# Where two batches of attention pairs are finished: moving pairs 12 and 13 of a fused retention and SwiGLU kernel behind the second tile's first quad

## The chip, the cores and the metric

The kernel runs on one core of one Trainium2 chip. Its engines are TensorE (PE in the profile, its weight loads PEld), VectorE (DVE), ScalarE (ACT), GpSimd (POOL) and SyncE (SP), which issues DMAs. Each engine works off its own instructions in order; an instruction waits for semaphores of the others. ScalarE and SyncE also issue DMAs, each in its own queue, marked ACTq and SPq. The metric is the time of one execution in microseconds (us), as a median over runs.

## The reference

Two blocks follow one another. First retention (attention without softmax) over 8 batches, 8 heads, 576 positions and head size 64:

```python
scores = (1 / sqrt(64)) * (q @ k.T)
gamma = 1 - 2.0 ** (-5 - head)
ret = scores * where(i >= j, gamma ** (i - j), 0)
attn = ret @ v
```

Its output becomes x, 4608 tokens of 512 features (heads side by side). Then a SwiGLU feed-forward block with 1536 hidden features:

```python
g = x @ w_gate
out = ((g * sigmoid(g)) * (x @ w_val)) @ w_out
```

q, k and v come as 32-bit floats, the three weights as 64-bit floats, which the kernel rounds to 32 bits itself.

## The kernel before, in words

**Pairs and ticks.** Retention is done for two heads at a time: 8 batches of 4 such pairs, 32 in all. A pair goes through three stages, and `tick(t)` (L482) does one stage for each of three pairs: for pair t-2 the values (`own_values`, `earlier_values`, `to_x`), for pair t-1 the states and scores (`new_states`, `scores`, `masked`), for pair t the transposes of q and k by VectorE and the scaling of kn by ScalarE (`transposes`, L402 and L404). Inside a tick TensorE does new_states, own_values, earlier_values and scores, and VectorE follows with to_x, masked and the two transposes. new_states writes the PSUM tile that masked of the tick before reads. A tick takes only pairs in the bounds that it is given (`lo`, `hi`).

**Loads.** `load(i)` (L248) fetches pair i: 14 DMAs by SyncE, eight for q and k, two for kn, four for v. `next_load(t)` asks for pair t+2.

**Tiles.** The feed-forward block takes the tokens in tiles: tile 0 has 512 tokens, tiles 1 to 4 have 1024. A tile needs the pairs of all batches that it touches: `needed(1)` is 14, so tile 1 needs pairs 0 to 11, whose last stage is in tick 13. Ticks for later pairs are spread among a tile's steps.

**Tile 0** is plain matmul: `up0(f, ...)` (L496) makes hidden block f of 12 in two PSUM banks (A and B, or C and E, in turn), `down0(f)` (L511) adds block f's part of the output in all four banks, and `out0` (L516) copies the banks out, three by VectorE and bankE by ScalarE (L522). Between the up0 calls VectorE rounds the weights (L372 to L375). The ticks 4 to 9 stand there at places written out in a table (`tick_at`).

**Tiles 1 to 4** save multiplications by sums of blocks, after tables (`UP`, `DOWN`) that give the sums for each step. A tile has three quads of 26 up steps (`up_step`, L648), each of eight matmuls (L663) into one of four banks, then 26 down steps (`down_step`, L688) of twelve matmuls (L697). An up step's result is read from its bank by ScalarE copies (L618) in steps 0 to 3, 10 and 11 of a quad and by VectorE (L621) in the others; a bank is written again three or four steps later, so that read must be done by then. Finished sums go through a silu by ScalarE (L678) and a product by VectorE (L681, L684). In tile 1 the work of all steps is on VectorE (`busy`), and the sums of x (`x_sums`, L630) run with the first quad: eight ahead of it, one in each of its first 13 steps. They are written over memory that tile 0 has done with: those of steps 0 to 3 over the last quarter of the down weights. Tile 1 also makes the sums of the up weights (`w_sums`, `first_sums`, mostly by GpSimd), and stores them for later tiles (L666, ScalarE's queue).

**Sums of the down weights.** `out_sums(qd)` (L544) lists 26 sums for each of three quarters of w_out. GpSimd makes each in one of six slots, and a DMA (L561) stores it to DRAM for later tiles, so a slot can be written again only when its store has landed. They are done in 27 groups of up to three. `sums_of(group, late)` (L743) issues the store at once by SyncE, or, if late, by ScalarE and up to three sums later. Before, the steps f = 7 to 11 of tile 0 do 3, 3, 3, 2 and 2 groups by SyncE, and the down steps the other 14 by ScalarE.

**Order.** The engines' order is the program's order (`manual_schedule`). `merge` (L715) interleaves lists evenly: element i of a list of n with offset d gets the place (i + d) / n. Before, tile 0's down steps are merged with ticks 10 to 13 at offset 0 and their next loads at 0.3. Tick 10 so comes ahead of the first down step, straight behind tick 9. In tile 1 the ticks 14 to 17 are merged with the 78 up steps and 18 to 21 with the 26 down steps. Tick 14 so comes ahead of step 0.

Of the kernel before, what the change touches and what calls it, by code (L numbers as in the profile page):

```python
# [149 lines left out]
def kernel(  # L150
# [35 lines left out]
    HP = H // 2  # L186
# [8 lines left out]
    NF = DF // P  # L195
    NQ = NF // 4
# [91 lines left out]
    NP = B * HP  # L288
# [193 lines left out]
    def tick(t, lo=HP, hi=NP):  # L482
        for fn, i in ((new_states, t - 1), (own_values, t - 2), (earlier_values, t - 2), (scores, t - 1),
                      (to_x, t - 2), (masked, t - 1), (transposes, t)):
            if lo <= i < hi:
                fn(i)

    def needed(n):

        last = (min(starts[n] + TW, NT) - 1) // S  # L490
        return last * HP + HP - 1 + 3
# [19 lines left out]
    def down0(f):  # L511
        for i, bank in enumerate(banks):
            nc.tensor.matmul(bank, hid0[f][:, ts(i, P)], w_dn[:, f // 4, f % 4].rearrange("p d x -> p (d x)"),
                             start=(f == down_order[0]), stop=(f == down_order[-1]))
# [12 lines left out]
    N = len(up)  # L527
# [100 lines left out]
    X_FIRST = 8  # L628

    def x_sums(n, lo, hi, vector):  # L630
        for op in x_ops[lo:hi]:
            add(nc.vector if vector or op[0] == "nad" else nc.gpsimd, op, x_view(n))
# [5 lines left out]
    def first_sums(qd):  # L638

        engines = [nc.scalar, nc.gpsimd, nc.vector, nc.gpsimd]  # L640
        for op, eng in zip(up[0][5], engines, strict=True):
            if op[0] == "neg":
                nc.scalar.mul(out=up_view(qd)(int(op[1])), in_=up_view(qd)(int(op[2])), mul=-1.0)
            else:
                add(eng, op, up_view(qd))
        w_sums(qd, 1)

    def up_step(n, qd, i):  # L648
        label, opens, xslot, _, wslot, _, ops = up[i]
        busy = n == 1  # L650
        if qd == 0:
            x_sums(n, X_FIRST + i, X_FIRST + i + 1, busy)
        if busy:
            if i > 1:
                w_sums(qd, i)
            w = up_view(qd)(wslot)
        else:
            w = operand()[:, 0:512].rearrange("p (g x) -> p g x", g=2)
        rhs = x_view(n)(xslot)
        b = bank(label, i == 0)  # L660
        for gv in range(2):
            for c in range(2):
                nc.tensor.matmul(b[:, gv * TB : (gv + 1) * TB], w[:, gv, ts(c, P)], rhs[:, c, :],  # L663
                                 start=(opens and gv == 0 and c == 0), stop=(c == 1), skip_group_check=True)
        if busy:
            nc.scalar.dma_start(out=up_ops[qd][i].rearrange("p (g x) -> p g x", g=2), in_=w)  # L666
            if i == 22 and qd + 1 < NQ:
                first_sums(qd + 1)
            if qd + 1 == NQ and i >= 22:
                for _ in range(3 if i == 22 else 5 if i == N - 1 else 0):  # L670
                    fetch()
        else:
            fetch()

        def result(o, src, negative, vector):
            s = io[:, (silus[0] % 4) * TB : (silus[0] % 4 + 1) * TB]
            silus[0] += 1
            nc.scalar.activation(out=s, in_=src[:, 0:TB], func=AF.Silu, scale=-1.0 if negative else 1.0)  # L678
            dst = hid[:, qd, o // 4, o % 4]
            if negative:  # L680
                nc.vector.scalar_tensor_tensor(out=dst, in0=src[:, TB : 2 * TB], scalar=-1.0, in1=s,  # L681
                                               op0=ALU.mult, op1=ALU.mult)
            else:
                (nc.vector if vector else nc.gpsimd).tensor_tensor(out=dst, in0=src[:, TB : 2 * TB], in1=s, op=ALU.mult)  # L684

        reads(ops, b, busy, result)
# [28 lines left out]
    def merge(*lists):  # L715
        merged = [((i + d) / len(l), j, f) for j, (d, l) in enumerate(lists) for i, f in enumerate(l)]
        for _, _, f in sorted(merged, key=lambda e: e[:2]):
            f()

    E = mybir.EngineType  # L720
    ctx.enter_context(tc.manual_schedule(engines={E.PE, E.DVE, E.Activation, E.Pool, E.SP}))
    ticks = lambda a, b: [lambda t=t: tick(t) for t in range(a, b)]

    for t in range(HP + 2):
        tick(t, 0, HP)
# [17 lines left out]
    def sums_of(group, late=False):  # L743
        def f():
            for make, store, slot, written in group:
                stores_until(3, written)
                make()
                waiting.append((slot, lambda store=store: store(nc.scalar if late else nc.sync)))
                if not late:
                    stores_until(0)  # L750
        return f


    def next_load(t):
        if t + AHEAD < NP:
            load(t + AHEAD)

    groups = [(qd, out_sums(qd)[i : i + 3]) for qd in range(NQ) for i in range(0, N, 3)]
    todo = [m for m in range(3, len(order))]
    plan = []  # L760
# [7 lines left out]
    tick_at = {2: 4, 3: 5, 5: 6, 7: 7, 10: 8, 11: 9}  # L768
    for f in range(2, NF):
        round_until({4: 12, 6: 13, 8: 14, 9: 15, 10: 16, 11: 17}.get(f, f + 2))  # L770
        plan.append(lambda f=f: up0(f, range(HP)))
        if f - 1 in tick_at:
            plan.append(lambda t=tick_at[f - 1]: next_load(t))
        if f in tick_at:
            plan.append(lambda t=tick_at[f]: tick(t))
        for _ in range(3 if f < 10 else 2):
            if f >= (7, 10, NF)[groups[0][0]]:
                plan.append(sums_of(groups.pop(0)[1]))
    assert not todo
    for f in plan:  # L780
        f()
    next_load(9)
    tail = []
    for m, f in enumerate(down_order):
        tail.append(lambda f=f: down0(f))
        if m == 6:
            tail.append(lambda: first_sums(0))
        if m > 8:
            tail.append(lambda m=m: x_sums(1, 3 * (m - 9), min(3 * (m - 8), X_FIRST), True))
        for _ in range(-(-len(groups) // (len(down_order) - m))):  # L790
            tail.append(sums_of(groups.pop(0)[1], True))
    last = ticks(10, needed(1))
    merge((0.0, last), (0.3, [lambda t=t: next_load(t) for t in range(10, needed(1))]), (0.5, tail))
    stores_until(0)
    out0()
    done = needed(1)
    for n in range(1, NTILE):
        upto = needed(n + 1) if n + 1 < NTILE else done
        cut = (done + upto) // 2
        for a, b, steps in ((done, cut, [lambda qd=qd, i=i: up_step(n, qd, i) for qd in range(NQ) for i in range(N)]),  # L800
                            (cut, upto, [lambda i=i: down_step(n, i) for i in range(N)])):
            merge((0.0, ticks(a, b)), (0.2, [lambda t=t: next_load(t) for t in range(a, b)]), (0.5, steps))
        done = upto

# [29 lines left out]
```

## Time and profile before

| what | value |
|---|---|
| median of 5 runs | 1120.79 us (1116.61 to 1122.41) |
| the profiled execution: time, span | 1120.92 us, 1119.2 us |
| mean granted TensorE clock | 0.989 |
| tile 0's first down step starts | 155.55 us |
| tile 1's first up step, first down step start | 212.47 us, 384.36 us |
| tile 2's first up step starts | 467.42 us |
| sum stores (dn<-rest): by ScalarE, by SyncE | 40, 38 |

The span runs from the first instruction to the last. A timeline row has start and length in us, engine, line, operation, what is written and read, shapes and count; in brackets the idle time of the engine ahead of it and what ended it. "Granted clock" is the share of TensorE's full clock that was granted in a stretch.

### The profile page before, as it was taken

The numbers are of one execution on the slowest core, as the hardware profiler recorded it, in microseconds if no ns is written. First come the engines' busy times: TensorE is split into PE (matmuls) and PEld (weight loads), VectorE is DVE, ScalarE is ACT, GpSimd is POOL, SyncE is SP. The second block draws the span as 40 slices with busy tenths as digits, with TensorE's granted clock in tenths as the row PEclk, the third lists the DMA queues.
The fourth block names the chain that finished last, engine by engine and source line by source line (L and its number), as shares of the span: only waits on it lengthen the run. The fifth ranks groups of instructions, "written<-read, shape, count | busy, mean of one in ns | idle before, by whom it ended". The sixth has DMA issues, their size and how long they took to land.

```text
span 1119.2 us, 17258 instructions
## 1 busy us (share of the span) xinstructions
PE 1076.9 (96%) x6372; PEld 884.5 (79%) x6372; DVE 658.6 (59%) x1081; ACT 249.0 (22%) x510; POOL 380.3 (34%) x337
## 2 busy tenths in 40 slices
PE   5899979898999999999999999999999999999998
PEld 4545455686888788888888888888888888888887
DVE  2689953678576865744544767444447465343654
ACT  3454500112221211113122110221321011322210
POOL 1002467352435402461213306622223076122504
PEclk9999989998999999999999999999999999999999
DMA  9989858875465587676558577554564555555653
GB/s 214 230 215 248 224 152 202 203 200 145 150 178 166 198 205 208 187 191 175 136 168 226 152 178 219 166 151 133 151 180 140 160 172 154 154 151 151 192 159 101
DMA packets 304195, 198.31 MB, mean 177 GB/s; under 512 B 219632, under 2 KB 247280, under 8 KB 304112
## 3 DMA queue, kind: packets, MB, share of 16 engines
q1 hardware_dynamic: 270208, 150.70, 50.9%
q10 hardware_dynamic: 33904, 46.51, 12.6%
q8 instruction: 51, 0.84, 0.3%
q14 instruction: 32, 0.26, 0.1%
HBM read 157.04 MB, written 40.11 MB: 176 GB/s over the span
## 4 chain that ended last, share of the span: by engine, by line
PE 74%; DVE 11%; DMA 6%; issue 2%; SPq 2%; POOL 2%; ACT 1%; ACTq 0%; DVEq 0%; POOLq 0%
PE bankC L663 11%; PE bankA L663 11%; PE bankE L663 10%; PE bankB L663 10%; PE bankB L697 6%; PE bankA L697 6%; PE bankC L697 6%; PE bankE L697 6%; DVE rest L621 2%; DMA dn<-rest 2%; PE sc L442 2%; PE xo L416 2%; DVE rest L373 1%; PE xo L433 1%; POOL rest L539 1%
## 5 line engine op out<-in xcount | busy, mean ns | idle before, releaser
L621 POOL TENSOR_TENSOR rest<-rest 128x512 f32<-128x512 f32 x56 | 79.4, 1424 | 310.2 <-DVE rest L621 285.2
L678 ACT ACTIVATE io<-rest 128x256 f32<-128x256 f32 x180 | 74.9, 417 | 383.6 <-DVE rest L621 324.2
L539 POOL TENSOR_TENSOR arena<-arena 128x512 f32<-128x512 f32 (+1 forms) x72 | 113.4, 1588 | 106.8 <-DMA up<-arena 21.9
L663 PE MATMUL bankC<-rest,arena 128*128 128x256 f32 x544 | 130.9, 384 | 5.9 <-DVE rest L621 5.9
L663 PE MATMUL bankA<-rest,arena 128*128 128x256 f32 x544 | 130.8, 384 | 5.1 <-ACT rest L618 3.3
L539 POOL TENSOR_TENSOR rest<-rest 128x256 f32<-128x256 f32 (+1 forms) x86 | 82.6, 977 | 126.5 <-DVE rest L375 94.1
L663 PE MATMUL bankE<-rest,arena 128*128 128x256 f32 x512 | 121.3, 380 | 3.7 <-DVE rest L621 3.7
L663 PE MATMUL bankB<-rest,arena 128*128 128x256 f32 x512 | 121.3, 380 | 0.0
L663 PEld LDWEIGHTS bankC<-rest,arena 128*128 128x128 f32 x544 | 103.9, 192 | 21.3 <-issue 5.9
L663 PEld LDWEIGHTS bankA<-rest,arena 128*128 128x128 f32 x544 | 104.0, 192 | 20.5 <-ACT rest L618 3.7
L684 POOL TENSOR_TENSOR arena<-rest,io 128x256 f32<-128x256 f32 x72 | 51.9, 726 | 174.6 <-ACT io L678 174.6
L663 PEld LDWEIGHTS bankE<-rest,arena 128*128 128x128 f32 x512 | 96.9, 190 | 17.8 <-issue 2.6
L663 PEld LDWEIGHTS bankB<-rest,arena 128*128 128x128 f32 x512 | 97.0, 190 | 13.6 <-DVE arena L534 0.2
L621 DVE TENSOR_TENSOR rest<-bankE,rest 128x512 f32<-128x512 f32 x72 | 48.8, 686 | 63.9 <-PE bankE L663 46.2
L621 DVE TENSOR_TENSOR rest<-bankC,rest 128x512 f32<-128x512 f32 x72 | 48.8, 685 | 62.0 <-PE bankC L663 40.7
L621 DVE TENSOR_TENSOR rest<-bankA,rest 128x512 f32<-128x512 f32 x72 | 48.8, 686 | 58.4 <-PE bankA L663 42.7
L621 DVE TENSOR_TENSOR rest<-bankB,rest 128x512 f32<-128x512 f32 x72 | 48.8, 686 | 54.1 <-PE bankB L663 39.4
L681 DVE SCALAR_TENSOR_TENSOR arena<-rest,io 128x256 f32<-128x256 f32 x84 | 56.3, 672 | 29.1 <-ACT io L678 29.1
L697 PE MATMUL bankB<-arena 128*128 128x256 f32 x252 | 58.2, 381 | 0.0
L697 PE MATMUL bankA<-arena 128*128 128x256 f32 x252 | 58.1, 380 | 0.0
L697 PE MATMUL bankC<-arena 128*128 128x256 f32 x252 | 58.0, 380 | 0.0
L697 PE MATMUL bankE<-arena 128*128 128x256 f32 x252 | 57.9, 379 | 0.0
(147 smaller groups left out, 1620.4 us busy)
## 6 DMA issues: line engine op xcount, KB each, us to landing
arena<-up SPq DMA_DIRECT2D x234, 256.0 KB, 2.6
arena<-dn SPq DMA_DIRECT2D x104, 384.0 KB, 3.4
up<-arena ACTq DMA_DIRECT2D x78, 256.0 KB, 2.7
out_dram<-rest SPq DMA_DIRECT2D x32, 256.0 KB, 2.9
qk<-in_q_dram SPq DMA_DIRECT2D x112, 72.0 KB, 3.1
qk<-in_k_dram SPq DMA_DIRECT2D x112, 72.0 KB, 3.0
v<-in_v_dram SPq DMA_DIRECT2D x62, 128.0 KB, 3.0
kn<-in_k_dram SPq DMA_DIRECT2D x58, 128.0 KB, 2.9
```

The costliest lines, as they stand in the source:

```text
L373: nc.vector.scalar_tensor_tensor(out=top, in0=top, scalar=-(1 << 31), in1=dst, op0=ALU.bitwise_and, op1=ALU.bitwise_or)
L416: nc.tensor.matmul(xo[half[hl], ts(c, P)], s["v"][:, c, hl, :], ret[:, hl, ts(c, P)], start=(c == 0), stop=(c == 0), skip_group_check=True)
L433: nc.tensor.matmul(o[half[hl]], state[half[hl], c - 1, :], s["qT"][half[hl], c * P : c * P + w], start=False, stop=True, skip_group_check= ...
L442: nc.tensor.matmul(sc[hl][:, ts(c, P)], kT[half[hl], ts(c, P)], qT[half[hl], ts(c, P)], start=True, stop=True)
L539: eng.tensor_tensor(out=dst, in0=srcs[0], in1=srcs[1], op=ALU.add if op[0] == "add" else ALU.subtract)
L621: eng.tensor_tensor(out=at(op[1]), in0=at(op[2]), in1=at(op[3]), op=ALU.add if op[0] == "add" else ALU.subtract)
L663: nc.tensor.matmul(b[:, gv * TB : (gv + 1) * TB], w[:, gv, ts(c, P)], rhs[:, c, :], start=(opens and gv == 0 and c == 0), stop=(c == 1), s ...
L678: nc.scalar.activation(out=s, in_=src[:, 0:TB], func=AF.Silu, scale=-1.0 if negative else 1.0)
L681: nc.vector.scalar_tensor_tensor(out=dst, in0=src[:, TB : 2 * TB], scalar=-1.0, in1=s, op0=ALU.mult, op1=ALU.mult)
L684: (nc.vector if vector else nc.gpsimd).tensor_tensor(out=dst, in0=src[:, TB : 2 * TB], in1=s, op=ALU.mult)
L697: nc.tensor.matmul(b[:, m * TB : (m + 1) * TB], lhs[:, qd, ts(m, P)], w[:, qd], start=(opens and qd == 0 and m == 0), stop=(qd == NQ - 1), ...
```

## The change

Ticks of tile 0 are now bounded at pair 12 (`FIRST = needed(1) - 2 = 12`). Pairs 12 and 13 thus do none of their stages in ticks 12 and 13 there; ticks 12 and 13 are called a second time in tile 1 with the bounds 12 to 32, and do that part. In the first quad of tile 1 no tick stands any more, only the loads of pairs 12 and 13, after its steps 6 and 14. Ticks 12 to 16 are merged with the other 52 up steps and 17 to 21 with the 26 down steps, each with its next load at offset 0.2. In tile 0 the down steps are not merged any more: ticks 10, 11, 12 and 13 come after the 2nd, 4th, 7th and 9th of them, and the load of pair 11 after the first. The groups of down-weight sums: 3 each at f = 7 to 9 by SyncE, none at f = 10, 3 at f = 11 by ScalarE (late), and the other 15 among the down steps by SyncE, stored at once.

```diff
@@ -719,7 +719,6 @@
 
     E = mybir.EngineType
     ctx.enter_context(tc.manual_schedule(engines={E.PE, E.DVE, E.Activation, E.Pool, E.SP}))
-    ticks = lambda a, b: [lambda t=t: tick(t) for t in range(a, b)]
 
     for t in range(HP + 2):
         tick(t, 0, HP)
@@ -751,6 +750,9 @@
         return f
 
 
+
+    FIRST = needed(1) - 2
+
     def next_load(t):
         if t + AHEAD < NP:
             load(t + AHEAD)
@@ -772,33 +774,41 @@
         if f - 1 in tick_at:
             plan.append(lambda t=tick_at[f - 1]: next_load(t))
         if f in tick_at:
-            plan.append(lambda t=tick_at[f]: tick(t))
-        for _ in range(3 if f < 10 else 2):
+            plan.append(lambda t=tick_at[f]: tick(t, HP, FIRST))
+        for _ in range(3 if f < 10 or f + 1 == NF else 0):
             if f >= (7, 10, NF)[groups[0][0]]:
-                plan.append(sums_of(groups.pop(0)[1]))
+                plan.append(sums_of(groups.pop(0)[1], f + 1 == NF))
     assert not todo
     for f in plan:
         f()
-    next_load(9)
-    tail = []
+    tick_at = {1: 10, 3: 11, 6: 12, 8: 13}
     for m, f in enumerate(down_order):
-        tail.append(lambda f=f: down0(f))
+        down0(f)
+        if m == 0:
+            next_load(9)
+        if m in tick_at:
+            tick(tick_at[m], HP, FIRST)
         if m == 6:
-            tail.append(lambda: first_sums(0))
+            first_sums(0)
         if m > 8:
-            tail.append(lambda m=m: x_sums(1, 3 * (m - 9), min(3 * (m - 8), X_FIRST), True))
+            x_sums(1, 3 * (m - 9), min(3 * (m - 8), X_FIRST), True)
         for _ in range(-(-len(groups) // (len(down_order) - m))):
-            tail.append(sums_of(groups.pop(0)[1], True))
-    last = ticks(10, needed(1))
-    merge((0.0, last), (0.3, [lambda t=t: next_load(t) for t in range(10, needed(1))]), (0.5, tail))
+            sums_of(groups.pop(0)[1])()
     stores_until(0)
     out0()
-    done = needed(1)
+    done = FIRST
+    ticks = lambda a, b: [lambda t=t: tick(t, FIRST, NP) for t in range(a, b)]
     for n in range(1, NTILE):
         upto = needed(n + 1) if n + 1 < NTILE else done
         cut = (done + upto) // 2
-        for a, b, steps in ((done, cut, [lambda qd=qd, i=i: up_step(n, qd, i) for qd in range(NQ) for i in range(N)]),
-                            (cut, upto, [lambda i=i: down_step(n, i) for i in range(N)])):
+        ups = [lambda qd=qd, i=i: up_step(n, qd, i) for qd in range(NQ) for i in range(N)]
+        if n == 1:
+
+            for i in range(N):
+                ups.pop(0)()
+                if i in (6, 14):
+                    load(FIRST + i // 14)
+        for a, b, steps in ((done, cut, ups), (cut, upto, [lambda i=i: down_step(n, i) for i in range(N)])):
             merge((0.0, ticks(a, b)), (0.2, [lambda t=t: next_load(t) for t in range(a, b)]), (0.5, steps))
         done = upto
```

## The prediction

> **What bounds the kernel now.** I read the page's first table, then TensorE in order of time, then busy time by stretch.
>
> ```profile
> PE 1076.9 (96%) x6372; PEld 884.5 (79%) x6372; DVE 658.6 (59%) x1081; ACT 249.0 (22%) x510; POOL 380.3 (34%) x337
> ```
>
> TensorE is the bound, so only its idle or slowed time can be won. The busy time by stretch (start:end, length, busy time and instructions of each engine, granted clock) says where that is.
>
> ```profile
> 138.80:155.60 16.80, 9.22 (x146) 8.30 (x145) 13.18 (x27) 0.38 (x1) 13.04 (x17) 0.80 0.44 148
> 155.60:212.50 56.90, 56.90 (x387) 31.38 (x385) 26.04 (x58) 4.58 (x9) 35.48 (x47) 1.00 0.77 183
> 212.50:277.60 65.10, 54.81 (x283) 46.20 (x282) 51.94 (x83) 13.70 (x30) 22.19 (x17) 0.90 0.69 188
> 277.60:328.90 51.30, 49.11 (x281) 42.64 (x280) 35.79 (x59) 12.63 (x27) 21.20 (x16) 1.00 0.50 155
> 328.90:380.70 51.80, 49.65 (x283) 42.37 (x283) 35.52 (x59) 12.80 (x28) 19.68 (x15) 1.00 0.57 176
> 380.70:467.40 86.70, 86.70 (x672) 75.74 (x672) 59.98 (x98) 10.33 (x21) 25.63 (x15) 1.00 0.78 210
> ```
>
> The rows are: ticks 9 and 10; the down steps of tile 0; tile 1's first, second and third quad; tile 1's down steps. I price them by two units from the timeline. An undisturbed up step starts 1.727 us after the one before (281.05 to 282.77). A whole tick between two steps adds 3.82 (step starts 251.75 and 257.30, less 1.73). Lost time is then:
> - ticks 9 and 10: 16.75 - 2 x 3.82 = **9.1 us**;
> - first quad: 65.1 - 26 x 1.727 - 3.82 = **16.4**;
> - other two quads: 102.9 - 52 x 1.727 - 2 x 3.82 = **5.5**;
> - the down steps of both tiles: nothing.
>
> So 31 us lie where the change works. The TensorE timeline shows the stalls.
>
> ```profile
> 150.30 1.10 PE L423 MATMUL mix<-v,kn 128*64 128x64 f32 x15 [6.48 <-issue]
> 217.76 1.89 PE L663 MATMUL bankE<-rest,arena 128*128 128x256 f32 x8
> 222.93 3.78 PE L663 MATMUL bankA<-rest,arena 128*128 128x256 f32 x8 [3.28 <-ACT rest L618]
> 236.10 1.99 PE L663 MATMUL bankE<-rest,arena 128*128 128x256 f32 x8 [1.47 <-DVE rest L621]
> 268.28 3.75 PE L663 MATMUL bankC<-rest,arena 128*128 128x256 f32 x8 [5.53 <-DVE rest L621]
> ```
>
> A step of eight matmuls takes 1.89 us, but 3.78 and 3.75 behind the two long stalls: the clock (0.80 and 0.90 in those stretches) falls behind a stall and costs 2.4 us more (from 268.28, four steps take 9.32 instead of 6.91). Stalls of 1.47 and 2.19 us cost no clock.
>
> The Trainium skill (TensorE: Matmul & The Clock Gate, section on the HAM clock gate) has the clock halved after an idle window of some 3.4 us; here 3.28 us was enough. By its rule that stall would not have been charged, so the sum for it would be 2.4 smaller; the stall of 4.2 forecast below is charged by both.
>
> **The change part by part.**
>
> *Tick 10 behind two down steps.* Now tick 10 follows tick 9 at once, and its first matmuls overwrite what VectorE still reads:
>
> ```profile
> 146.39 0.68 DVE L506 TENSOR_TENSOR arena<-bankE,io 128x512 f32<-128x512 f32 x1
> 149.29 0.91 DVE L454 SCALAR_TENSOR_TENSOR state<-state,tab,mix 128x64 f32<-128x64 f32 x3
> ```
>
> VectorE is late with weight rounding and ends tick 9's states at 150.2. Afterwards TensorE leaves tick 9 at 143.8 and has two down steps (eight matmuls of 0.4375 us, 3.5 us each) as cover: three banks' worth until 146.4, a wait of 0.7 for bankE (read until 147.1), and tick 10 starts at 151.5, behind 150.2. The stall of 6.48 and its slow clock go; the 1.10 us ahead of tick 9 stays. Lost: 1.1 + 0.7 instead of 9.1, or **-7.3 us**.
>
> What is late next? Pair 10's loads stand on SyncE behind 23 sum stores, which end at 154.9; six of these move behind them, so they start near 148.3 and end 7.9 us later (as 155.0 to 162.9), at 156.2. Tick 10's transposes start at about 158: covered. ScalarE must then scale kn for tick 11, behind the nine stores that it now gets from f = 11. GpSimd does those sums at 146.7 to about 157.6, so kn is ready near 159.5; tick 11 comes at 162.4. If that cover is gone, up to 3 us come back.
>
> *Pairs 12 and 13 out of tile 0, and SyncE for the stores.* The matmuls of tick 14 (3.82) and of tick 13's front (0.6 + 1.3, less overlap 1.8) only change place; tile 1 then starts at 212.5 - 7.3 - 5.6 = **199.6**. What they dragged along goes: four loads of 14 DMAs each leave SyncE's tail queue, and ScalarE loses 31 of 40 stores. Its timeline shows what that is worth.
>
> ```profile
> 203.49 11.44 ACTq L561 DMA_DIRECT2D dn<-rest  x12
> 216.50 0.58 ACT L522 COPY rest<-bankE 128x512 f32<-128x512 f32 x1 [12.56 <-DMA dn<-rest]
> 220.80 1.12 ACT L404 ACTIVATE kn<-kn,tab 128x256 f32<-128x256 f32 x2 [3.72 <-DMA kn<-in_k_dram]
> 221.83 0.56 ACT L618 COPY rest<-bankA 128x512 f32<-128x512 f32 x1
> ```
>
> ScalarE first waits for the stores, then for tick 14's kn, and only at 221.83 clears bankA, which step 4 needs. With no tick there and no store ahead, its copies follow each step, as in quad 2 (first at 279.52, behind a step ending 279.48). The 3.28 us stall goes.
>
> By the skill (DMA: Bandwidth & Descriptors, "Issuing engines are not separate DMA queues") another issuing engine saves only issue time; by that alone this part is worth 0.5 us per store off the path, nothing. What I price is the order: the work behind the stores on ScalarE.
>
> *First quad without ticks.* Removing a stall shows what is late next: VectorE.
>
> ```profile
> 226.82 0.69 DVE L621 TENSOR_TENSOR rest<-bankA,rest 128x512 f32<-128x512 f32 x1 [2.50 <-PE bankA L663]
> 233.70 1.75 DVE L539 TENSOR_TENSOR rest<-rest,x_odd 128x512 f32<-128x512 f32 x1
> 262.99 0.22 DVE L474 TENSOR_TENSOR rest<-mix,tab 128x64 f32<-128x64 f32 x1
> 267.48 0.65 DVE L621 TENSOR_TENSOR rest<-bankC,rest 128x512 f32<-128x512 f32 x1
> ```
>
> From step 4's bank (226.82) to the end of step 18's work (262.99) it needs 36.2 us, 31.7 of them busy, the rest waits of 0.48 for ScalarE's silus. TensorE covers these steps in about 26. Then tick 15 takes 4.5 before step 19's bank is read, which step 22 needs. Afterwards, with tile 1 starting at T: step 4 ends at T + 4 x 1.727 + 1.89 = T + 8.8, the chain of 36.2 and the read of 0.65 follow, and step 22 starts at T + 45.8 instead of T + 38.0. So 7.8 us stay lost, and the stall before step 22 (about 4.2, the rest falling at steps 9, 20 and 21) is long enough for the slow clock, 2.4. Lost 10.2 instead of 16.4: **-6.2 us**. Its ends: -12 if VectorE runs without its long forms (1.75 beside the usual 0.69), 0 if the chain starts no earlier than now.
>
> *Five ticks in the last two quads.* They fall before steps 26 (transposes alone), 36, 47, 57 and 68. Step 36 is harmless: that part of the quad is copies by ScalarE, and VectorE now idles 1.8 us there. Every quad has its burst at steps 18 to 21 of it, and step 22 waits: 2.19 us in one quad and 1.81 in the next, though VectorE had caught up before the latter. Tick 14 now comes inside that wait, before step 21 of its quad: its 3.82 us of TensorE cover it, then 4.5 us of VectorE leave waits of about 0.9 and 0.4: 1.3 for 2.5, or -1.2. Tick 16 comes just ahead of the burst: 4.5 + 7.55 us of VectorE from 365.85 end at 377.9, against step 22 at 375.3: 2.6, which may bring the slow clock (2.4 at one in three). With tick 15's 0.4 that is 3.8 for 2.9, or +0.9. Sum **-0.3**, ends -3 and +6.
>
> *Five ticks in the down steps instead of four*: 26 steps at no loss, VectorE 60.0 of 86.7 us, plus 4.5 per tick. **0**; if VectorE stalled there as in the quads, +2.
>
> **Sum**: -7.3 - 6.2 - 0.3 = -13.8. The profiled execution took 1120.92 us (span 1119.2 and 1.7 around it); the median shown is 1120.79, so both give **1107 us**.
>
> **Rivals.**
>
> *The sums end too late* (slower). Tile 1's second and fourth step overwrite tile 0's last down weights, so VectorE waits there for the last sum stores. They may land until about T + 7 (206.6) for nothing. SyncE reaches its 43 stores at about 164, behind two loads. At the 0.72 us per store of 136.0 to 148.2 (17 stores), with 3 us of weight sums and 4 of waiting, they end near 202. But ScalarE's 40 stores needed 52 us (162.8 to 214.9), 1.30 each: then the last lands at about 222, 15 us late, and with the clock's 2.4 the time is 1120.9 - 13.8 + 17.4 = **1124.5**. It decides from 1.0 us per store on, and above 1.25 eats all. Against it: those stores stood behind kn scalings that waited for loads, and here nothing stands between.
>
> *Only the tail is won.* VectorE's chain starts late, by the stores at some 1.0 us each, or the burst is worse: 1120.9 - 7.3 = **1114**.
>
> *VectorE keeps up better* when GpSimd's sums fall elsewhere; no slow clock: -7.3 - 10 - 2 = **1101**.
>
> *The change moves nothing*: the waits return at the new places, **1120**.
>
> **How the numbers follow.** The forecast (1103 to 1111) 0.56; only the tail 0.16; better 0.12; nothing 0.07; slower 0.09. A difference under 0.3% (3.4 us) can't be told from none in this kernel: faster 0.84, same 0.07, slower 0.09. The range takes in the first three: 1100 to 1117.
>
> **What would show it.** Right: no stall between ticks 9 and 10, tile 1 starting near 199.6, ScalarE copying bankA within a us of step 0, one long VectorE stall at the first quad's step 22. Wrong: VectorE waiting for sum stores in tile 1's first steps, a stall above 4 us in the third quad, or any in the down steps.

## The result and the profile after

The changed kernel takes 1118.42 us (median of 31 runs, 1112.67 to 1123.38), the kernel before 1121.0 (52 runs). The ratio is **0.9971**, with a 95% interval of 0.9961 to 0.9981: 0.3% faster, some 3 us of the 14 that were forecast, and outside the range of 1100 to 1117. The profiled execution took 1116.65 us (span 1114.9), 4.3 less than that of before.

First the stretches (start:end, length, busy time and instructions of each engine, granted clock, DMA): tile 0's down steps, tile 1's three quads, tile 1's down steps.

```profile
143.39:200.70 57.31, 56.00 (x351) 29.89 (x349) 33.11 (x64) 2.55 (x5) 40.17 (x50) 1.00 0.51 140
200.70:258.38 57.68, 49.67 (x209) 41.06 (x209) 41.28 (x57) 10.98 (x24) 30.17 (x26) 0.94 0.67 197
258.38:312.78 54.40, 51.46 (x316) 44.22 (x317) 41.60 (x70) 14.24 (x33) 21.04 (x16) 1.00 0.65 178
312.78:374.45 61.67, 57.29 (x424) 49.12 (x425) 45.51 (x82) 15.54 (x35) 26.45 (x18) 1.00 0.65 184
374.45:463.10 88.65, 88.65 (x673) 76.88 (x673) 59.06 (x98) 9.93 (x20) 19.04 (x12) 0.98 0.78 205
```

The clock column shows two stretches with a slowed clock, the first quad (0.94) and, new, the down steps of tile 1 (0.98). TensorE's timeline has the stalls.

```profile
146.79 1.12 PE L513 MATMUL bankE<-rest,arena 128*128 128x512 f32 x2 [0.56 <-DVE arena L506]
...
212.18 3.78 PE L663 MATMUL bankA<-rest,arena 128*128 128x256 f32 x8 [3.90 <-ACT rest L618]
...
250.93 1.97 PE L663 MATMUL bankC<-rest,arena 128*128 128x256 f32 x8 [2.88 <-DVE rest L621]
...
307.86 0.45 PE L663 MATMUL bankA<-rest,arena 128*128 128x256 f32 x1 [1.71 <-DVE rest L621]
...
361.40 0.89 PE L663 MATMUL bankA<-rest,arena 128*128 128x256 f32 x3 [1.82 <-DVE rest L621]
...
374.45 4.51 PE L697 MATMUL bankA<-arena 128*128 128x256 f32 x12 [2.17 <-DMA arena<-dn]
```

The wait of 6.48 us between ticks 9 and 10 is gone, and in the tail 0.56 is left. But step 4 of tile 1 (212.18) still waits 3.90 us for ScalarE, with the slow clock behind it (eight matmuls in 3.78 us). And the first down step (374.45) waits 2.17 us for the fetch of its weights, and its twelve matmuls then take 4.51 us at the slow clock, where nothing had stood before.

Why step 4 waits is read off the engines before it. GpSimd's timeline:

```profile
159.27 2.22 POOL L539 TENSOR_TENSOR rest<-rest 128x256 f32<-128x256 f32 x3
172.36 0.72 POOL L536 TENSOR_TENSOR rest<-rest 128x256 f32<-128x256 f32 x1 [10.87 <-DMA dn<-rest]
```

SyncE's queue (number of DMAs at the end of each line; the lines left out are further DMAs of the two loads):

```profile
147.99 3.37 SPq L278 DMA_DIRECT2D qk<-in_q_dram  x4
154.10 2.11 SPq L278 DMA_DIRECT2D qk<-in_k_dram  x4
...
161.28 2.14 SPq L278 DMA_DIRECT2D qk<-in_q_dram  x4
...
169.99 41.46 SPq L561 DMA_DIRECT2D dn<-rest  x43
```

VectorE, then ScalarE:

```profile
208.48 1.20 DVE L539 TENSOR_TENSOR rest<-x_odd 128x512 f32<-128x512 f32 x1 [6.73 <-POOL rest L539]
211.96 0.69 DVE L539 TENSOR_TENSOR rest<-x_odd,rest 128x512 f32<-128x512 f32 x1 [2.29 <-DMA dn<-rest]
```

```profile
211.05 0.59 ACT L618 COPY rest<-bankA 128x512 f32<-128x512 f32 x1 [4.88 <-DMA dn<-rest]
```

SyncE works off the loads of pairs 10 and 11 from 147.99 to 169.89 and comes to the first store of the 43 at 169.99. GpSimd has filled its six slots by 161.5 and stands still for 10.87 us. From 172.36 it is busy 31.26 of 36.76 us, up to its last sum at 209.12. VectorE's sums of x overwrite the weights that these sums read, and so wait until 208.48 and, for the last stores, 211.96. ScalarE's own stores wait too: the DMAs of both queues take eight completion semaphores in turn, and a DMA is issued only when the one before it on its semaphore has landed. ScalarE's third and fourth output store (205.15 and 207.93) each go out right after a SyncE sum store has landed (205.07 and 207.86), its first up store (210.68) likewise (210.66), and the copies of bankA stand behind that.

The same coupling holds up the load of pair 10. The nine late sum stores of f = 11 go out on ScalarE while SyncE issues this load:

```profile
149.94 6.66 ACTq L561 DMA_DIRECT2D dn<-rest  x9
```

SyncE's waits between 147 and 171 us (time in total, times, longest):

```profile
SPq L278 <- DMA dn<-rest: 3.1, 2, 2.7
SPq L259 <- DMA dn<-rest: 1.8, 2, 1.1
```

The DMA at 154.10, for one, takes the semaphore of a store that ScalarE issued at 151.85 and that landed at 154.08. Three such waits (2.7, 0.8 and 1.1 us) are 4.6 of the 13.2 us that this load takes, from 147.99 to 161.17.

For the comparison of all runs, the same stretches from TensorE's starts (us): A tile 0's first matmul to its first down step, B its down steps, C to E tile 1's quads (E to the first down step), F tile 1's down steps. From tile 2's first step to the last matmul all kernels take 647.9, e1 excepted.

| kernel | A | B | C | D | E | F | sum | ratio to before, 95% interval |
|---|---|---|---|---|---|---|---|---|
| before | 115.74 | 56.92 | 65.12 | 51.32 | 55.44 | 83.06 | 427.6 | 1 |
| after | 103.77 | 57.31 | 57.68 | 54.41 | 61.67 | 88.65 | 423.5 | 0.9971 [0.9961, 0.9981] |
| e1 | 104.19 | 57.63 | 59.65 | 53.76 | 60.29 | 86.99 | 422.5 (+2.3 later) | 0.9963 [0.9943, 0.9983] |
| e2 | 104.11 | 56.07 | 54.70 | 54.31 | 62.05 | 86.96 | 418.2 | 0.9901 [0.9878, 0.9923] |
| e3 | 105.50 | 61.39 | 82.95 | 51.27 | 55.52 | 83.06 | 439.7 | 1.0103 [1.0080, 1.0126] |
| e4 | 116.03 | 53.95 | 57.64 | 53.89 | 62.21 | 86.96 | 430.7 | 1.0005 [0.9986, 1.0024] |
| e5 | 104.69 | 56.59 | 56.65 | 53.91 | 61.41 | 86.96 | 420.2 | 0.9958 [0.9942, 0.9974] |
| e6 | 103.58 | 57.56 | 61.61 | 53.89 | 62.85 | 88.65 | 428.1 | 0.9975 [0.9963, 0.9987] |
| e8 | 103.89 | 56.55 | 61.12 | 53.88 | 62.01 | 86.96 | 424.4 | 0.9965 [0.9945, 0.9984] |
| e10 | 104.49 | 57.06 | 59.85 | 55.36 | 58.84 | 86.99 | 422.6 | 0.9946 [0.9925, 0.9966] |
| e11 | 107.27 | 57.12 | 57.01 | 57.30 | 58.14 | 86.99 | 423.8 | 0.9940 [0.9917, 0.9963] |
| e12 | 103.64 | 57.70 | 56.83 | 57.16 | 58.14 | 86.99 | 420.5 | 0.9929 [0.9916, 0.9942] |
| e13 | 104.94 | 56.98 | 53.63 | 53.69 | 58.55 | 86.99 | 414.8 | 0.9875 [0.9862, 0.9887] |
| e14 | 107.20 | 57.11 | 62.28 | 53.89 | 62.51 | 88.65 | 431.6 | 0.9988 [0.9970, 1.0006] |

A stretch is one execution's, the ratio that of medians. Where a slow clock falls by chance (see the end) a stretch moves by 1.7 us, and A, whose program hardly differs from after on (e4 excepted), goes from 103.6 to 107.3, mostly by stalls (0.8 us of them in e6, 3.9 in e11). The profiled execution need not be a typical one: that of e5 is its fastest (1111.49 us), those of e3, e6 and e14 are their slowest (1135.87, 1121.94 and 1126.93). So single stretches are read together with the stalls in them, and the time by the ratios.

### The profile page after: what moved, and what is told of

The parts are those of the page before. It is cut to its first block, busy times and chain, and to the rows that moved or that the text cites. A ratio compares the mean times of both kernels' runs of the same rounds, so it can differ in the third digit from the quotient of the medians.

```text
span 1114.9 us, 17263 instructions
## 1 busy us (share of the span) xinstructions
PE 1077.5 (97%) x6372; PEld 882.5 (79%) x6372; DVE 661.1 (59%) x1081; ACT 248.7 (22%) x510; POOL 385.8 (35%) x337
## 4 chain that ended last, share of the span: by engine, by line
PE 70%; DMA 11%; DVE 9%; POOL 4%; issue 2%; SPq 2%; ACT 2%; ACTq 0%; DVEq 0%; POOLq 0%
PE bankA L663 10%; PE bankE L663 10%; PE bankC L663 10%; PE bankB L663 9%; PE bankA L697 6%; PE bankC L697 6%; PE bankB L697 6%; PE bankE L697 6%; DMA up<-arena 3%; DVE rest L621 3%; DMA dn<-rest 2%; POOL rest L539 2%; PE sc L442 2%; PE xo L416 2%; DMA qk<-in_k_dram 1%
## 5 line engine op out<-in xcount | busy, mean ns | idle before, releaser
L539 POOL TENSOR_TENSOR arena<-arena 128x512 f32<-128x512 f32 (+1 forms) x72 | 116.1, 1626 | 95.4 <-DMA up<-arena 41.2
L681 DVE SCALAR_TENSOR_TENSOR arena<-rest,io 128x256 f32<-128x256 f32 x84 | 53.1, 635 | 29.2 <-ACT io L678 29.2
```

The source lines that it names most:

```text
L539: eng.tensor_tensor(out=dst, in0=srcs[0], in1=srcs[1], op=ALU.add if op[0] == "add" else ALU.subtract)
```

## The experiments

### The two halves of the change alone (e4, e3)

e4 is the change of the pairs alone: tile 1 as in the kernel after, the tail of tile 0 as before (merged, stores of the sums by ScalarE, ticks bounded at 12, no loads of pairs 12 and 13).

```diff
-        down0(f)
-        if m in tick_at:
-            tick(tick_at[m], HP, FIRST)
+        tail.append(lambda f=f: down0(f))
...
-            sums_of(groups.pop(0)[1])()
+            tail.append(sums_of(groups.pop(0)[1], True))
+    last = [lambda t=t: tick(t, HP, FIRST) for t in range(10, needed(1))]
+    merge((0.0, last), (0.5, tail))
```

> The other part alone: pairs 12 and 13 behind tile 1's first quad, the tail of tile 0 merged and its sums stored by ScalarE as before the change (without the loads that moved). Theory: the stall between ticks 9 and 10 is back (+7.3 us against the change), which gives the sums 7 us more and starts four groups earlier, so step 4 does not wait (-6.5): about 1119. Rival (the sums are late whatever the order): step 4 waits 3 to 4 us as well, 1125.

Measured: 1121.3 us, 1.0005 [0.9986, 1.0024]. TensorE's timeline has the old stall in the tail back:

```profile
149.22 0.57 PE L423 MATMUL mix<-v,kn 128*64 128x64 f32 x5 [6.48 <-issue]
```

The pairs alone win nothing that can be told: the first quad is 7.5 us shorter than before, and D to F, which take up the ticks, are 13.2 longer, while B is only 3.0 shorter. Step 4 doesn't wait, as the theory said; its time of about 1119 did not come.

e3 is the tail alone: ticks behind the down steps, stores by SyncE, but all pairs up to 13 finished in tile 0, with their loads.

```diff
-    FIRST = needed(1) - 2
+    FIRST = needed(1)
...
-            tick(tick_at[m], HP, FIRST)
+            tick(tick_at[m])
+            next_load(tick_at[m])
```

> One part alone: fixed places for ticks 10 to 13, each with its next load, and SyncE for the sum stores there, while pairs 12 and 13 stay in ticks 12 to 15 and tile 1 is as before the change. Theory: the stall between ticks 9 and 10 goes (7.3 us), but four loads on SyncE among the stores let the sums end later still, so step 4 of tile 1 waits 4 us or more: about 1118, between 1116 and 1122. Rival (the pairs are what matters, the tail's order nothing): as before, 1121.

Measured: 1132.92 us, 1.0103 [1.0080, 1.0126], slower by 1.0%, and far outside the theory's 1116 to 1122. SyncE's queue now holds four more loads between the stores, and GpSimd waits 10.72, 9.01, 6.10 and 10.38 us for stores to land; VectorE's first sum of x that waits for them starts at 236.8. TensorE, in the first quad:

```profile
239.13 0.79 PE L663 MATMUL bankE<-rest,arena 128*128 128x256 f32 x1 [12.12 <-POOL arena L539]
```

So the parts do not add: A is 10.2 us shorter than before (12.0 in the kernel after), and the first quad gives back 17.8. By these waits, what SyncE carries ahead of the sum stores decides; moving the pairs pays by taking four loads out of that queue.

### Are the late sums what the first quad loses? (e2)

Here GpSimd's sums of the third quarter of w_out are left out (the stores remain and write what lies in the slots), so the output isn't the reference's.

```diff
-                for op in terms(ops):
+                for op in terms(ops) if qd < 2 else []:
```

> The changed kernel without GpSimd's sums of the third quarter of w_out; their 26 stores stay in place (they store what the slots hold). Theory (step 4 waits, over ScalarE's copies, for the last sum stores): GpSimd ends some 20 us earlier, the 3.90 us stall of step 4 and its slow clock (2.6) go, VectorE's chain starts 7 us earlier, the stall at step 22 grows from 2.88 to about 4 with a slow clock: 5 to 7 us less in all, about 1112. Rival (ScalarE is held by its own output stores or by pair loads): step 4's stall stays and the time is 1117 to 1119.

Measured: 1110.7 us, 0.9901 [0.9878, 0.9923], so 0.7% below the kernel after. The stall at step 4 is gone. What remains in the first quad is the stall that VectorE sets at step 22:

```profile
246.29 0.91 PE L663 MATMUL bankC<-rest,arena 128*128 128x256 f32 x3 [2.88 <-DVE rest L621]
```

Tile 1 starts at 200.26 here, so step 22 starts 46.0 us later; the prediction's chain of VectorE had 45.8. In the kernel after it is 50.2 (250.93 - 200.70). Leaving out sums also frees VectorE from working beside GpSimd (see the end); that this isn't what counts is seen in e13 below, which keeps all sums and has 45.05.

### ScalarE's order or the sums? (e6)

```diff
+    kept = []
...
-            nc.scalar.dma_start(out=out[i * P : (i + 1) * P, :], in_=o)
+            kept.append(lambda i=i, o=o: nc.scalar.dma_start(out=out[i * P : (i + 1) * P, :], in_=o))
...
+        first = busy and qd == 0 and i < 4
+        store = lambda: nc.scalar.dma_start(out=up_ops[qd][i].rearrange("p (g x) -> p g x", g=2), in_=w)
...
+        if first:
+            store()
+            if i == 3:
+                for f in kept:
+                    f()
```

> The kernel after, with ScalarE's four output stores of tile 0 and the up stores of steps 0 to 3 issued behind step 3's copies instead of ahead of them, so that no copy of bankA to bankE waits for a store of ScalarE. It separates the two reasons that the late sum stores had in the trace of after. Theory (VectorE's first sums of x wait by themselves for the last sum stores, until 212): the 3.90 us stall at step 4 goes or shrinks below 1, but VectorE's chain to step 22 starts no earlier, and the time lost is lost there: 0 to 1.5 us less than after, 1117 to 1118. Rival (ScalarE's order was the only cause): step 4 starts 3.9 us earlier, no slow clock, step 22 comes 4 to 6 us earlier, 1112 to 1114.

Measured: 1117.87 us, 0.9975 [0.9963, 0.9987], as after. VectorE's wait for the sums stands (this kernel's lines are two higher):

```profile
210.36 1.19 DVE L541 TENSOR_TENSOR rest<-x_odd 128x512 f32<-128x512 f32 x1 [7.92 <-POOL rest L541]
```

Step 4's stall went; stalls of 0.51 and 2.46 us at steps 5 and 6 and of 1.02 and 1.19 at later ones came for it, and step 22 starts 53.2 us after tile 1's first step, in the slowest of its executions. The edit also delays up stores, so part of these stalls may be its own. But VectorE's wait did not need ScalarE's order: that was the place of the stall, not its cause.

### Who stores the sums (e8, e5)

e8 gives the sums of the first two down steps to ScalarE, e5 those of all.

```diff
-            sums_of(groups.pop(0)[1])()
+            sums_of(groups.pop(0)[1], m < 2)()
```

> The sums of the first two down steps (of tile 0) are stored by ScalarE, late; the others by SyncE as in the kernel after. Theory (GpSimd stands idle for 10.9 us, from 161.5 to 172.4, because its six slots come free only when SyncE has worked off the loads of pairs 10 and 11, and the sums then end at 209 instead of some 200): GpSimd goes on over that time, the sums end at 200 to 204, the stall of 3.90 us at tile 1's step 4 and its slow clock go, and the time falls by 5 to 6 us, to about 1113. A little may come back (up to 1.5 us) if ScalarE's scaling of kn for tick 11 stands behind these stores. Rival (the rate of 0.96 us per store is what ends the sums late, not their start): six stores fewer on SyncE, 6 us earlier at the last store, but ScalarE's stores slow those of SyncE by as much, and step 4 still stalls by more than 3 us: 1118.

Measured: 1115.87 us, 0.9965 [0.9945, 0.9984]. GpSimd's long idle stretch is gone, but step 4's gain is lost one step earlier:

```profile
211.33 0.89 PE L663 MATMUL bankE<-rest,arena 128*128 128x256 f32 x3 [2.56 <-ACT rest L522]
```

ScalarE's copy of bankE stands behind its output stores, the first of which (208.44) waited for a SyncE sum store that landed at 208.37. The theory's 5 to 6 us did not come; the rival's time is within the interval, though not its 3 us at step 4. The intervals of e8 and after overlap.

```diff
-            sums_of(groups.pop(0)[1])()
+            sums_of(groups.pop(0)[1], True)()
```

> All sums of tile 0's down steps are stored by ScalarE, late, as in the kernel before; ticks, pairs and places as in the kernel after. It isolates the part of the change that gives the stores to SyncE. Theory (in the kernel after the stores on SyncE start late, behind two loads, and on ScalarE they would start at once, but at about 1.3 us each as before, 45 of them from 158 on): the sums end at about 215, 6 us later than after; step 4 stalls by about 6 more, and the last two stores stand ahead of ScalarE's copies: 1122 to 1126. Rival (the 1.3 us of before came only from kn scalings in between, which waited for loads): about 0.9 each, an end near 200, no stall at step 4: 1112 to 1114, faster than the kernel after.

Measured: 1117.03 us, 0.9958 [0.9942, 0.9974]. The theory of 1.3 us per store fell: in the profiled execution ScalarE issues the last sum store at 201.7, step 4 has no stall, and step 22 starts 48.0 us after tile 1's first step. This execution is the fastest of ten, 5.5 us below their median, so how often step 4 is free isn't known. By the medians, giving the stores to SyncE, which the prediction had counted as the gain in the first quad, wins nothing that can be told over giving them to ScalarE, and the rival's 1112 to 1114 did not come either. GpSimd's timeline names what is late next:

```profile
209.91 1.35 POOL L539 TENSOR_TENSOR arena<-arena 128x512 f32<-128x512 f32 x1 [10.19 <-DMA up<-arena]
```

The sums of the up weights wait for the first store of one, which stands on ScalarE behind the sum stores and four output stores.

### The load of pair 18, and the places of the ticks (e1, e10, e11)

e1 moves only the load of pair 18 from the last steps of the third quad behind the first down step.

```diff
+            loads = range(a, b) if n > 1 else range(a, b - 1) if a == FIRST else range(a - 1, b)
-            merge((0.0, ticks(a, b)), (0.2, [lambda t=t: next_load(t) for t in range(a, b)]), (0.5, steps))
+            merge((0.0, ticks(a, b)), (0.2, [lambda t=t: next_load(t) for t in loads]), (0.5, steps))
```

> The changed kernel with one edit: the load of pair 18, which stood among tile 1's last up steps, comes behind the first down step, so SyncE issues the fetches of the down operands first. Theory (SyncE's order): the first down step's wait of 2.17 us and the slow clock behind it (4.52 us for a step of 2.86, so 1.7) go, and the time falls by 3.8 us, to about 1114.6. Rival (the fetches wait for landings or for the ring whatever stands ahead of them): the first down step still waits about 2 us and the time stays at 1118.4.

Measured: 1117.4 us, 0.9963 [0.9943, 0.9983]. The stall at the first down step and its slow clock went, as the theory of SyncE's order said: E and F are 3.0 us shorter. In tile 2, though, 2.3 came back, and the time can't be told from that of after: an output store of tile 1 now stands behind loads on SyncE, lands at 470.19, and the copy into the same place waits for it.

```profile
471.41 0.48 PE L663 MATMUL bankC<-rest,arena 128*128 128x256 f32 x1 [1.16 <-ACT rest L618]
```

e10 keeps the load but moves it forward, with the ticks: ahead of steps 26, 28, 36, 53 and 62, away from VectorE's bursts.

```diff
+            quiet = {0: 12, 2: 13, 10: 14, 27: 15, 36: 16}
+            for s in range(2 * N):
+                if s in quiet:
+                    tick(quiet[s], FIRST, NP)
+                ups.pop(0)()
+                if s in quiet:
+                    next_load(quiet[s])
...
```

> Ticks 12 to 16 stand ahead of steps 26, 28, 36, 53 and 62 of tile 1 instead of 26, 36, 47, 57 and 68, each with its next load right behind it; so no tick falls within the burst of VectorE's work at steps 18 to 21 of a quad, and pair 18 is loaded some 10 us earlier, ahead of the fetches of the down weights. Theory (stalls of the two last quads come from ticks that fall in or just ahead of the burst; the stall of 2.17 us and the slow clock at the first down step come from the load of pair 18 ahead of the first fetch): the stalls of 1.71, 1.23 and 1.82 us shrink to under 2 us together (3 won), and the first down step starts without a stall (3.9 won); 2 of it may be given back in tile 2, where tile 1's last output store stands behind loads, as in the run with only that load moved. Time 1112 to 1115. Rival (the bursts stall by themselves, since VectorE is the bound of a quad with or without a tick in it): only the down step's part is won, and given back: 1117 to 1119.

Measured: 1115.23 us, 0.9946 [0.9925, 0.9966], just above the theory's 1112 to 1115. SyncE's queue shows the fetches of the down weights free of loads:

```profile
366.53 13.45 SPq L589 DMA_DIRECT2D arena<-dn  x9
```

The first down step starts without a stall, nothing comes back in tile 2, and E and F are 4.5 us shorter. The bursts still stall by 2.16 and 1.81 us, so of the ticks' part the rival was nearer.

> The two edits before together (first two groups of sums stored by ScalarE; ticks at the quiet steps). Theory: they lie in different stretches, and the gains add: 8 to 11 us less than the kernel after, 1107 to 1111. Rival (an earlier start of tile 1's chain only lengthens the stall at step 22 of the first quad, which VectorE's chain sets): the first edit is lost again there, and the sum is the second edit's alone, 1113 to 1116.

e11 puts e8 and e10 together (their two diffs). Measured: 1114.76 us, 0.9940 [0.9917, 0.9963]. The gains don't add: step 3 stalls 2.09 us for the same copy of bankE as in e8.

### Both late places mended (e12, e13, e14)

e12 is e5 and e10 together. e13 changes one line more, and e14 has this line alone in the kernel after:

```diff
-            nc.scalar.dma_start(out=out[i * P : (i + 1) * P, :], in_=o)
+            nc.sync.dma_start(out=out[i * P : (i + 1) * P, :], in_=o)
```

> The stores of tile 0's tail sums by ScalarE, late, and the ticks of tile 1 at the quiet steps: the two earlier edits that each left out a different stretch's loss. Theory (with the stores off SyncE the two queues no longer wait for each other and no copy waits at step 4; with pair 18's load ahead of the fetches the first down step has no stall; both stay): about 3.3 from the first (from the first matmul of tile 0 to tile 2's first step 420.2 instead of 423.5 in the kernel after) and 1 to 3 from the second: 419 to 417, 1112 to 1114. Rival (what the first part wins in the first quad is lost in the second one, since VectorE sets the pace of both): 422, 1115 to 1116.

> As the run before in this list, and the four output stores of tile 0 by SyncE instead of ScalarE. With the sums' stores on ScalarE, its stores of the up sums stand behind these four, GpSimd waits 10.2 us for the first of them to land (until 209.8), and steps 6, 9 and 10 of tile 1 stall by 1.05, 0.81 and 0.75 on what it makes. Theory (the queue's order is what GpSimd waits for): the first up store goes out some 2 us earlier, these three stalls shrink to under 1 us together, step 22 starts 46 to 47 us after tile 1's first step instead of 48.0: 1 to 2 us less than the run before. Rival (step 22 is set by VectorE's own work): no difference, within 0.5 us.

> The kernel after with one edit: the four output stores of tile 0 by SyncE, the sums' stores by SyncE too, ticks as in after. It asks whether the gain of the run with both stores exchanged (1107) needs the sums' stores on ScalarE. Theory (the sums end late because SyncE starts their stores behind two loads, GpSimd's idle stretch of 10.9 us stays, and VectorE's sums of x wait until some 212 whoever stores the output): 1116 to 1118, step 22 still 49 to 51 us after tile 1's first step. Rival (the output stores on ScalarE, each behind a sum store's landing, were what delayed the up stores and with them GpSimd and VectorE): 1111 to 1113, step 22 at 46 to 47 us.

Measured: e12 1113.34 us, 0.9929 [0.9916, 0.9942]; e13 **1107.33 us, 0.9875 [0.9862, 0.9887]**, faster than both kernels of this study; e14 1120.76 us, 0.9988 [0.9970, 1.0006]. e12 came as its theory said; e14 came out above both its theory (1116 to 1118) and its rival (1111 to 1113).

In e12 GpSimd still waits for the first up store:

```profile
213.99 1.38 POOL L539 TENSOR_TENSOR arena<-arena 128x512 f32<-128x512 f32 x1 [10.48 <-DMA up<-arena]
```

In e13 it doesn't wait in the tail for 10.87 us nor here for 10.48:

```profile
167.96 0.72 POOL L539 TENSOR_TENSOR rest<-rest 128x256 f32<-128x256 f32 x1 [3.38 <-DMA dn<-rest]
...
207.10 1.54 POOL L539 TENSOR_TENSOR arena<-arena 128x512 f32<-128x512 f32 x1 [5.35 <-DMA up<-arena]
```

Its first quad, and the one long stall in it:

```profile
200.74:254.37 53.63, 47.80 (x209) 40.14 (x208) 43.09 (x60) 11.82 (x25) 24.41 (x18) 0.97 0.66 195
```

```profile
245.79 0.77 PE L663 MATMUL bankC<-rest,arena 128*128 128x256 f32 x1 [2.88 <-DVE rest L621]
```

Step 22 comes 45.05 us after tile 1's first step, and the last sum ends at 201.7 instead of 209.1. In e14 the sums are as late as in the kernel after, whoever stores the output; GpSimd, then VectorE:

```profile
177.09 0.72 POOL L536 TENSOR_TENSOR rest<-rest 128x256 f32<-128x256 f32 x1 [11.14 <-DMA dn<-rest]
```

```profile
215.02 1.20 DVE L539 TENSOR_TENSOR rest<-x_odd 128x512 f32<-128x512 f32 x1 [7.87 <-POOL rest L539]
```

So the line that wins 6.0 us (1113.34 to 1107.33) behind sum stores by ScalarE wins nothing behind sum stores by SyncE: there it removes a wait that isn't the last. (e12 and e13 also have the ticks at the quiet steps, which e14 hasn't. None of these ticks stands in the first quad; whether the second quad's part needs them was not run.) e13's theory expected 1 to 2 us of it; by the table's sums it is 5.7: 3.2 in the first quad and 3.5 in the second, with 1.0 given back elsewhere. Of the second quad's 3.5, 1.7 is a slow clock that a stall of 2.27 us met in e12 and one of 2.17 missed in e13, which is luck. Another 1.5 is tick 13, and the last 0.2 shorter waits. Between two up steps the tick adds 3.6 us in e12 and 2.1 in e13, because in e12 it waits for ScalarE's scaling of kn and for VectorE's transpose:

```profile
262.39 1.08 PE L423 MATMUL mix<-v,kn 128*64 128x64 f32 x16 [0.67 <-ACT kn L404]
263.80 0.33 PE L439 MATMUL mix<-qT,kT 64*64 64x64 f32 x4 [0.33 <-DVE kT L402]
```

## Why the prediction was wrong

By the profiled executions, -13.8 was forecast and -4.3 came. The number lies nearest to the rival in which the change moves nothing (1120), but that isn't what happened: the tail's gain came, and later stretches gave part of it back. Of the signs named, the right ones came in the tail, and two of the wrong ones behind it: VectorE waits for sum stores in tile 1's first steps, and a down step stalls. ScalarE copies bankA not within a us of step 0, but some 10 us after it starts (211.05). Measured from the first matmul of tile 0, so that a differing start does not count:

| term | forecast | measured | how |
|---|---|---|---|
| tail: tick 10 behind two down steps | -7.3 | -6.0 | A + B: 161.08 for 172.66, less 5.6 of moved work |
| first quad | -6.2 | -3.6 | C: 57.68 for 65.12, less tick 15's 3.82 |
| last two quads | -0.3 | +1.2 | lost 6.7 for 5.5 |
| five ticks in the down steps | 0 | +3.8 | stall 2.17; F 88.65 instead of 86.99 |

**The tail was right in its mechanism.** The stall of 6.48 us went, tick 10 starts at 151.28 (151.5 forecast), and the waits ahead of tick 9 and for bankE are 0.93 and 0.56 (1.1 and 0.7). Tile 1 starts at 200.70 (199.6); 0.75 of this is a wait that the forecast did not have, for VectorE's copy of bankA.

**The first quad failed in its premise, not in its chain.** The chain of VectorE was right: forecast 45.8 us to step 22, measured 46.0 with a third of the sums left out and 45.05 in e13. It started late, though, and the step that failed is the one priced under "the sums end too late": SyncE was to reach the stores at 164 and work them off at 0.72 us each, until 202. It reached them at 169.99, because the loads ahead of them took 13.2 and 8.6 us where 7.9 each was taken; the last store landed at 213.54 (206.6 would have cost nothing). Of the first load's 5.3 us more, 4.6 are the waits for ScalarE's stores of f = 11, which the change itself had put there; this is read off the trace, no run leaves them out. The price per store (0.96 measured, 41.46 / 43) wasn't SyncE's: GpSimd is busy 85% of that time (31.26 of 36.76), so the pace was that of the sums themselves. What was overlooked is that GpSimd, with six slots, can't run ahead of a queue that hasn't begun; its 10.87 us of idle time are what is late. The rival had asked the right question and set its decision by the wrong number, a rate instead of a start. It went half way; in e3, where the sums end some 28 us later still (237.4; 23.5 later if both are counted from the first down step), it took the whole gain and 1% more.

**The gain put down to "ScalarE loses 31 of 40 stores" was not one.** With all of these stores back on ScalarE (e5) the time does not rise: its 41 stores take 41.6 us (160.47 to 202.08), 1.0 each instead of 1.30. Two of the four kn scalings that stood among them before have moved to tile 1, which may be why; that isn't shown. The order argument held for another pair of DMAs: the four output stores ahead of the up stores. The Trainium skill (DMA: Bandwidth & Descriptors, "Issuing engines are not separate DMA queues") lets another issuing engine save only issue time. e5 alone would agree with that; e13 against e12, four DMAs exchanged for 6.0 us, does not: what counted there is the work that stood behind the DMAs.

**Last two quads:** tick 14 left 1.71 and 1.23 us (0.9 and 0.4 forecast), tick 16 1.82 (2.6), tick 15 0.39 (0.4). The sum is off by 1.5 us; the slow clock that was feared did not come.

**The down steps, put at 0, were costed by VectorE alone.** This is the largest miss, 3.8 us. The fifth tick of the last two quads brings its load along. The load of pair 18 stands on SyncE from 353.75 to 370.20 (16.5 us instead of the 7.9 of before), and the fetches of the down weights stand behind it: first issued at 370.31, landed at 374.32. The prediction followed a moved step's DMAs through SyncE's queue in the tail, and not here. e1 and e10 show it from both sides: with this load moved either way, the stall and the slow clock are gone.

The terms account for -4.6, the stretches for -4.1: tick 13's front was priced at 1.8 us where it left and takes 2.06 where it went (273.99 to 277.78, less 1.73), and the rest is rounding. The first matmul comes 0.2 us earlier, which makes -4.3. By the ratio of the medians it is 0.29%, 3.3 us, 1 less than the profiled executions.

e13's 1107 us equal the forecast only in sum: its tail is worse than forecast, its first quad better, and its ticks stand elsewhere.

**What stays open:** how much e5's edit alone is worth (its interval and that of after overlap, as do those of e1, e8 and e10), what e13 would take with the ticks as in after, what the sums would do without ScalarE's stores of f = 11, and whether loads 10 and 11 placed behind the first sum stores would do as well as ScalarE's stores; the last three were not run.

## What to carry to other kernels

When a step is moved, follow its DMAs through the queue of the engine that issues them, and ask of a producer with few buffers when its first buffer comes free, not only how fast the queue runs once it has begun. A stall's last releaser (here ScalarE's copy) may be only the place: free it, and see whether the time moves before building on it. Two waits that end together have to be removed together: each of the two exchanges of queues, alone in the kernel after, won nothing that could be told from none, and both together, with the ticks at quiet steps, came to 1.25% below the kernel before. What the ticks add to that was not separated.

## What the runs showed of the hardware

**The clock goes by a fixed raster.** In every trace the granted clock changes only at multiples of 3.413 us from its first fall (33.95 us in after; there 1.0, 52.0, 54.0, 100.0 and 101.0 of them, up to 480 us). Between 100 and 480 us of all 14 traces, a full clock was halved for the next such window after each of the 30 windows in which TensorE idled 2.02 us or more, and after none of those with up to 1.94; a halved clock stayed so if the next window had 0.68 us of idle time or more and rose again at up to 0.51. So a stall of 2.17 us in one window (374.45 in after) costs 1.7 us more, and one of 2.88 us that is cut by a boundary (250.93: 0.95 and 1.94) nothing, while the same 2.88 in e13 did. The prediction's price of 2.4 for every long stall was too coarse. The Trainium skill (TensorE: Matmul & The Clock Gate, "The HAM clock gate") has a free-running window of 3.413 us, which these traces show too; an idle window is its condition for the half clock, and here some 60% of one was enough.

**The start moves by more than the change won.** Tile 0's first matmul begins at 37.8 to 43.0 us of the span in these 14 traces, with the same program ahead of it. Two profiled executions of kernels are therefore compared from there on, not by their spans.

**GpSimd and VectorE slow each other.** While both work on sums, VectorE's 128x512 sums take 1.20 us instead of 0.69 (208.48 and 211.96 above), and GpSimd's 128x256 sums up to 1.17 instead of 0.72.
